# Turning expert 0's first rows earlier, casting two weights later, and filling both banks of a PSUM pair in an attention and mixture-of-experts kernel

## The chip, the core and the metric

The kernel runs on one core of a Trainium2 chip. The metric is device time in microseconds, the median of several runs. A core has five engines that each work through a queue of their own, strictly in order: TensorE (PE, matrix products; its weight loads are listed apart as PEld), VectorE (DVE), ScalarE (ACT), GpSimd (POOL) and SyncE (SP, which here only issues DMA transfers). They meet through counting semaphores: an instruction whose input is not ready holds up everything behind it on its own engine, and nothing on the others. Matrix products are summed in PSUM, which this kernel cuts into eight banks of 128 partitions x 512 float32 values.

## The reference

Three stages, each feeding the next, in float32 to the accuracy of float32:

```python
# 1 attention: batch 4, 8 heads, 576 tokens, head size 64
scores = (q @ k.T) / 8
keep   = scores >= scores.max(-1) - tau
attn   = softmax(where(keep, scores, -1e9));  x = attn @ v        # -> 2304 rows x 512
# 2 mixture of experts: 8 experts, two per row, hidden size 1024
noisy  = x @ w_gate + log1p(exp(x @ w_noise)) * noise
top2, top2_w = the two largest of noisy, softmax over the two
out[r] = sum over its two experts e of top2_w * (relu(x[r] @ w1[e]) @ w2[e])
# 3 a dense layer: hidden size 2048
h = out @ w_in;  y = (max(h, 0) + alpha * min(h, 0)) @ w_out
```

## The kernel before

Each operand of a product of the second and third stage, and of the scores, is held as two parts, a high one (a cast to fp32r) and a low one (the original minus the high part), and each product is summed from three: high x high, high x low, low x high. The high part is a cast on ScalarE, the low part a subtraction on VectorE or GpSimd.

**Attention.** The work is cut into 80 units (`units`): a batch, a chunk of 128 query rows, a pair of heads. A loop over iterations `i` overlaps four stages of different units, and what each engine does is emitted in exactly the order in which the loop is written (the schedule is manual). In iteration `i`:

- `t_mm(i-2, part)` transposes the masked exponentials of unit i-2 on TensorE in three parts (L418, L418, L420), and `a2` copies each part out of PSUM on ScalarE (L430, L430, L432);
- `d1(i, h)` on VectorE scales the scores of the two heads and takes their minimum (L377); `a1(i, h)` on ScalarE forms the two exponentials (L388);
- `d2(i-1, h)` on VectorE masks and sums the exponentials of the unit before (L401, two instructions); the transposes of the next iteration need them;
- `s_mm(i+1)` on TensorE computes the next unit's scores (L362) into two pairs of PSUM banks (`ps_s`); the pairs are freed by `d1(i)`;
- `pv(i-3)` multiplies with V (L454, L456).

After a chunk's last pair of heads a tile of 128 rows of attention output is complete: it is copied out of PSUM (`group_evac`, L479), turned (`turn_rows`, L497), divided by its sum (`scale_rows`, L505), and its gate logits are made (L522, L527, L531, L535, L538). Per group of one to three tiles the gate is then evaluated in a chain of small instructions (`gating`: L564 to L616) that ends in the rank of each row within its expert (L601 to L606 on TensorE, L612, L614 on VectorE) and in an indirect DMA that scatters the rows to their experts (L637).

**What is added to the loop by a table.** `put(i, f)` adds work `f` to iteration `i`; `put((i, p), f)` says where: p = -1 is ahead of `d2`, 0 ahead of `pv`, 1 at the end (the default). Two things are put there ahead of the next stage. The first eight weight blocks of expert 0 are loaded, cast (`w_hi`, L171 on ScalarE, 128 x 1024) and subtracted (`w_lo`, L177 on GpSimd, two instructions), one block in every second iteration from 66. And expert 0's first 256 rows, complete by then, are loaded in iteration 70 (`x_load`) and turned in iterations 78 and 79 (`x_split`: four transposes at L203 on TensorE, then the high half at L206 on ScalarE and the low half at L207 on VectorE).

**Fill.** From iteration 80 on there are no new scores to compute, and TensorE is given the first block of expert 0: eight sums of 12 matmuls over those 256 rows (`first_1`, L214, output 128 x 256), each followed by a cast with relu on ScalarE (`relu`, L224) and a subtraction on VectorE (L225), and then `first_2` (L232) for the second weight matrix. They run between and behind the last attention units, so that TensorE has work while the gate of the last tiles is evaluated and their rows are scattered and read back. The order is: sums 0 and 1 in iterations 80 and 81, sum 2, the last but one `pv`, sum 3 in iteration 82, and sums 4 to 7 among the last tile's logits and rank.

**PSUM.** `psum_s()` hands out a pair of banks as one tile, of which there are two; `psum_t()` one bank, of which there are three; `psum_v()` one. When a buffer comes round again, its first writer is made to wait for the last reader of what was there before. `first_1` takes a new pair for each sum and uses one bank of it, so the sums go round over two pairs, and sum f waits for the reads of sum f-2.

Of the kernel before, what the change touches and what calls it, by code (L numbers as in the profile page):

```python
# [14 lines left out]
HP = H // 2  # L15
# [4 lines left out]
NT = N // 128  # L20
# [5 lines left out]
DT = 2  # L26
# [7 lines left out]
def emit(tc, qt, kt, v, tau, wg, wn, noise, w1, w2, w_in, w_out, alpha, out):  # L34
# [8 lines left out]
    with (  # L43
# [59 lines left out]
        def psum_t(dt=FT):  # L103
            return pp.tile([128, 512], dt, name="ps_t", tag="t", bufs=3)
# [75 lines left out]
        xrows = {}  # L180
# [16 lines left out]
        def x_split(src, j, x, bank=None, is_blocked=True):  # L197
            ps = (bank or (psum_v, psum_t, psum_t, psum_t)[j])()
            if is_blocked:
                dve.transpose(ps, src)  # L200
            else:
                for c in range(HP):
                    pe.transpose(ps[:, c * 128:c * 128 + 128], src[:, c * 128:c * 128 + 128], ident)  # L203
            pv_ = ps.rearrange("p (c t) -> p c t", c=HP)
            xh = x[0][:, :, j * 128:j * 128 + 128]
            act.copy(xh, pv_)  # L206
            dve.tensor_tensor(x[1][:, :, j * 128:j * 128 + 128], pv_, f32(xh), op=OP.subtract)  # L207
# [139 lines left out]
        NU = len(units)  # L347
# [136 lines left out]
        def x_stages(T):  # L484
# [31 lines left out]

            def logits_mm():
                x = xts[T]
                ps = psum_t()
                g["lp"] = ps  # L520
                for c in range(HP):
                    pe.matmul(ps[c * 32:c * 32 + 32, :128], wcat[:, c], x[:, c], start=True, stop=True,  # L522
                              skip_group_check=True)
# [16 lines left out]
            if T < NT - 2:  # L540
                return [(0, 1, turn_rows), (1, -1, scale_rows), (1, 1, logits_mm), (2, -1, logits_copy),
                        (2, 1, flip), (3, -1, sum_)]
            return [(0, 1, rows), (1, 1, logits), (2, 1, flip), (3, 0, sum_), (0, 0, inverse)]

        def bc8(ap, n):
# [173 lines left out]
        put(64, w_load, 1)  # L719
        for n in range(W0):  # L720
            i = 66 + 2 * n
            put(i, w_hi, n)
            put(i + 1, w_lo, n, pool)
            put(i + 1, w_load, n + 2)
        for t in range(BLOCK0 // 128):
            put(70, x_load, 0, t)
            put(NU - 4 + DT + t, lambda t: x_split(xrows.pop((0, t)), t, X0, psum_t, False), t)

        fill = []

        def first_1(f):
            ps = psum_s()[:, f % 2]
            relu(f, BLOCK0, mm1(ps, BLOCK0, [0, 1, 2, 3], X0, f * 128), H0)

        g2 = {}
# [22 lines left out]
        for i in range(END):  # L758
# [32 lines left out]
            if outs:  # L791
                pv(iv)
                if units[iv][2] == HP - 1 or iv < SOLO:
                    T = group_evac(iv)
                    if T is not None:
                        todo = [(i + (1, 3, 5, 7, 2)[T] + d if T < 5 else i + 1 + d, p, f) for d, p, f in x_stages(T)]
                        if T == NT - 1:
                            last_rows.append(todo[0][2])
                            todo = [(i + 1, 0, todo[1][2]), (i + 1, 0, todo[4][2]), (i + 2, 0, todo[2][2]), (i + 2, 0, todo[3][2])]
                        if T == NT - 2:  # L800
                            todo = [(i + d, p, f[2]) for (d, p), f in zip(((1, 1), (1, 1), (2, 1), (2, 1)), todo)]
                        for t0, t1 in GROUPS:
                            if T == t1 - 1:
                                todo += [(i + {3: 8, NT - 1: 3, NT: 2}.get(t1, 4) + d, p, f) for d, p, f in gating(t0, t1)]
                        for j, p, f in todo:
                            put((j, p), f)
# [390 lines left out]
```

## Time and profile before

| | |
|---|---|
| median of 3 runs | 1158.6 us (1158.15 to 1158.63) |
| the profiled execution's own time | 1154.86 us |
| its span | 1153.1 us |
| TensorE busy | 1126.6 us, 98% |
| VectorE busy | 624.7 us, 54% |
| ScalarE busy | 529.1 us, 46% |
| GpSimd busy | 532.9 us, 46% |
| granted clock of TensorE | 0.9 or more in each of 40 slices |

Times in the profile run from the start of the span. The end of the span lies 1.8 us short of the execution's own time. Iteration 74 of the attention loop ends at about 270 us, iteration 78 at 287 us; the last attention product ends at 305 us, the gate of the last tile at 316 us, and the 1153 us end with the dense layer. A timeline row gives the start, the duration, the engine, the line and operation, the names and the shape, how many instructions of a kind were merged (x4), and in brackets the idle time of the engine just before the first of them with what ended it. Ends of matmuls are modelled and overlap the next start.

### The profile page before, as it was taken

The page shows a single profiled execution, that of the slowest core. Times are in us where ns is not written, and L with a number is a line of the kernel's source. Part 1 is how long each engine was busy: PE and PEld are TensorE (multiplying, and loading weights), DVE is VectorE, ACT ScalarE, POOL GpSimd, SP SyncE. Part 2 cuts the span into 40 slices and gives each one's busy share as a digit, 9 for nine tenths or more (in the row PEclk, how much of TensorE's full clock was granted, in tenths as well). Part 3 has the DMA queues.
Part 4 walks back from the last instruction along what each step waited for, and adds up shares of the span by engine and source line. Part 5 has one row for each costly group of instructions (what it writes and reads, how often), then busy time and mean ns, then how long its engine had stood idle before and what let it go on. Part 6 is the DMA issues. An engine that isn't in the chain of part 4 may idle for free. (4 is left out here: it accounts for less than half of the span.)

```text
span 1153.1 us, 20565 instructions
## 1 busy us (share of the span) xinstructions
PE 1126.6 (98%) x7754; PEld 973.3 (84%) x7754; DVE 624.7 (54%) x1332; ACT 529.1 (46%) x1039; POOL 532.9 (46%) x632
## 2 busy tenths in 40 slices
PE   7999999999899999999999999999999999999997
PEld 6887887877798989888989999898888888888886
DVE  6979999898534544454444444444443442442221
ACT  7978888788434444454444444433111121121111
POOL 7746545653525455545555455475332332332221
PEclk9999999999999999999999999999999999999999
DMA  6524222232356767677667675632321321320001
GB/s 211 150 87 126 92 96 84 93 120 93 147 157 190 201 193 197 191 186 196 192 187 200 195 202 168 188 120 69 77 53 50 75 57 45 80 57 20 24 1 39
DMA packets 156552, 141.50 MB, mean 123 GB/s; under 512 B 108576, under 2 KB 109216, under 8 KB 156448
## 3 DMA queue, kind: packets, MB, share of 16 engines
q1 hardware_dynamic: 150400, 120.91, 35.9%
q0 software_dynamic: 5760, 18.88, 4.9%
q8 instruction: 63, 1.03, 0.4%
q14 instruction: 41, 0.34, 0.1%
q10 hardware_dynamic: 288, 0.34, 0.1%
HBM read 97.11 MB, written 42.99 MB: 121 GB/s over the span
## 5 line engine op out<-in xcount | busy, mean ns | idle before, releaser
L214 PE MATMUL ps_t<-m_v,m_pair 128*128 128x384 f32 (+2 forms) x1216 | 220.1, 317 | 0.3 <-DVE m_v L207 0.3
L177 POOL TENSOR_TENSOR m_pair<-m_v,m_pair 128x512 fp32r<-128x512 f32 x114 | 151.7, 1352 | 129.5 <-ACT m_pair L171 107.5
L214 PEld LDWEIGHTS ps_t<-m_v,m_pair 128*128 128x128 f32 x1216 | 186.8, 190 | 8.4 <-DVE m_v L207 0.5
L1018 DVE TENSOR_SCALAR m_tmp<-ps_t,alpha_t 128x512 f32<-128x512 f32 (+1 forms) x80 | 55.7, 696 | 209.2 <-PE ps_t L214 207.3
L232 PE MATMUL ps_s<-m_pair,m_hh 128*128 128x512 f32 x528 | 167.4, 390 | 0.0
L225 DVE SCALAR_TENSOR_TENSOR m_gate<-ps_t,m_hh 128x384 fp32r<-128x384 f32 (+1 forms) x120 | 58.8, 492 | 169.4 <-ACT m_hh L224 169.3
L214 PE MATMUL ps_t<-m_v,m_early 128*128 128x256 f32 (+2 forms) x672 | 127.3, 320 | 0.0
L401 DVE SCALAR_TENSOR_TENSOR m_hh<-m_tmp,sm,m_hh 128x576 f32<-128x576 f32 x144 | 125.4, 903 | 0.0
L377 DVE TENSOR_SCALAR_CACHE_REDUCE m_tmp<-ps_s 128x576 f32<-128x576 f32 x144 | 105.2, 752 | 23.4 <-ACT m_last L432 9.0
L232 PEld LDWEIGHTS ps_s<-m_pair,m_hh 128*128 128x128 f32 x528 | 99.1, 188 | 20.3
L1023 POOL TENSOR_TENSOR m_v<-m_tmp,m_v 128x512 fp32r<-128x512 f32 x39 | 50.4, 1294 | 140.1 <-ACT m_v L1022 140.1
L214 PEld LDWEIGHTS ps_t<-m_v,m_early 128*128 128x128 f32 x672 | 105.9, 189 | 5.1 <-DVE m_v L207 0.4
L388 ACT ACTIVATE m_hh<-m_tmp,sm 128x576 f32<-128x576 f32 x144 | 105.6, 781 | 4.9 <-DVE m_tmp L377 4.8
L1022 ACT CAST m_v<-m_tmp 128x512 fp32r<-128x512 f32 x39 | 24.2, 621 | 173.7 <-DVE m_tmp L1019 173.7
L232 PE MATMUL ps_s<-m_pair,m_gate 128*128 128x512 f32 x264 | 102.9, 390 | 0.0
L362 PE MATMUL ps_s<-m_pair 64*128 64x288 f32 (+1 forms) x864 | 88.9, 318 | 12.2 <-DVE m_tmp L377 7.1
L224 ACT ACTIVATE m_hh<-ps_t 128x384 fp32r<-128x384 f32 (+1 forms) x120 | 52.7, 439 | 98.2 <-PE ps_t L214 96.8
L1023 POOL TENSOR_TENSOR m_gate<-m_tmp,m_gate 128x512 fp32r<-128x512 f32 (+1 forms) x41 | 44.1, 1076 | 115.8 <-ACT m_gate L1022 109.6
L1042 PE MATMUL ps_s<-m_pair,m_v 128*128 128x512 f32 x396 | 95.1, 389 | 0.0
L362 PEld LDWEIGHTS ps_s<-m_pair 64*128 64x128 f32 (+1 forms) x864 | 69.3, 192 | 26.0 <-DVE m_tmp L377 16.5
L1042 PE MATMUL ps_s<-m_pair,m_gate 128*128 128x512 f32 x360 | 88.3, 391 | 0.0
L1042 PEld LDWEIGHTS ps_s<-m_pair,m_v 128*128 128x128 f32 x396 | 74.3, 188 | 15.4
(233 smaller groups left out, 1981.3 us busy)
## 6 DMA issues: line engine op xcount, KB each, us to landing
m_v<-in_w_dram SPq DMA_DIRECT2D x64, 512.0 KB, 4.0
yg<-m_tmp SPq DMA_DIRECT2D x40, 256.0 KB, 3.3
m_tmp<-in_w_in_dram SPq DMA_DIRECT2D x16, 512.0 KB, 4.6
m_tmp<-in_w_out_dram SPq DMA_DIRECT2D x16, 512.0 KB, 5.2
m_early<-in_kt_dram SPq DMA_DIRECT2D x15, 320.0 KB, 3.4
yg<-m_gate SPq DMA_DIRECT2D x18, 256.0 KB, 2.1
m_rows<-xg SPq DMA_DIRECT2D x72, 64.0 KB, 2.8
out_dram<-m_tmp SPq DMA_DIRECT2D x18, 256.0 KB, 2.4
```

The source lines that it names most:

```text
L177: eng.tensor_tensor(WL[n][:, w], raw[:, w], f32(WH[n][:, w]), op=OP.subtract)
L214: pe.matmul(ps[:, :n], w[wc[d]][:, col:col + 128], x[xx][:, d, :n], start=(k == 0), stop=(k == 11))
L224: act.activation(h, ps, AF.Relu)
L225: dve.scalar_tensor_tensor(hs[1][:, f * n:f * n + n], ps, 0.0, f32(h), op0=OP.max, op1=OP.subtract)
L232: pe.matmul(ps, a[:, o:o + 128], ww[w][:, c:c + 512], start=(f == 0 and k == 0), stop=(f == nf - 1 and k == 2))
L362: pe.matmul(u["ps", h][:, x, :288], lhs, kk[r, o:o + 288], start=(k == 0), stop=(k == 2))
L377: dve.tensor_scalar(u["sp"][:, h].rearrange("p (a b) -> p a b", a=2), ps[:, :, :288], -0.125, None, op0=OP.mult, op1=OP.min, accum_out=u[" ...
L388: act.activation(u["em"][:, h], u["sp"][:, h], AF.Exp, bias=u["sm"][:, h:h + 1], scale=-1.0)
L401: dve.scalar_tensor_tensor(u["em"][:, h], u["sp"][:, h], sm[:, 2 + h:3 + h], u["em"][:, h], op0=OP.is_le, op1=OP.mult, accum_out=acc)
L1018: dve.tensor_scalar(g, ps, 0.0, alpha_t[:, f:f + 1], op0=OP.min, op1=OP.mult)
L1023: pool.tensor_tensor(h[:, n:2 * n], g, f32(h[:, :n]), op=OP.subtract)
L1042: pe.matmul(ps, h[x][:, t * 128:t * 128 + 128], ww[w][:, c:c + 512], start=(f == 0 and k == 0), stop=(f == 15 and k == 2))
```

## The change

Five edits to the table of work and to two helpers. Expert 0's two row tiles are turned at the end of iterations 74 and 78 instead of 78 and 79, and their halves are formed one iteration later at position -1, ahead of the masks `d2`. The casts, subtractions and following loads of weight blocks 6 and 7 move from iterations 78 to 81 to iterations 80 and 81. The logits of the last but one tile use a `ps_s` pair and have their stages listed one by one. `first_1` takes a new pair only for every second sum and puts two sums into its two banks.

```diff
@@ -201,6 +201,9 @@
             else:
                 for c in range(HP):
                     pe.transpose(ps[:, c * 128:c * 128 + 128], src[:, c * 128:c * 128 + 128], ident)
+            x_halves(ps, j, x)
+
+        def x_halves(ps, j, x):
             pv_ = ps.rearrange("p (c t) -> p c t", c=HP)
             xh = x[0][:, :, j * 128:j * 128 + 128]
             act.copy(xh, pv_)
@@ -516,7 +519,7 @@
 
             def logits_mm():
                 x = xts[T]
-                ps = psum_t()
+                ps = psum_s()[:, 0] if T == NT - 2 else psum_t()
                 g["lp"] = ps
@@ -540,6 +543,9 @@
             if T < NT - 2:
                 return [(0, 1, turn_rows), (1, -1, scale_rows), (1, 1, logits_mm), (2, -1, logits_copy),
                         (2, 1, flip), (3, -1, sum_)]
+            if T == NT - 2:
+                return [(0, 1, turn_rows), (0, 1, logits_mm), (1, -1, logits_copy), (1, 0, scale_rows),
+                        (1, 1, flip), (1, 1, sum_)]
             return [(0, 1, rows), (1, 1, logits), (2, 1, flip), (3, 0, sum_), (0, 0, inverse)]
@@ -719,17 +725,28 @@
         for n in range(W0):
             i = 66 + 2 * n
-            put(i, w_hi, n)
-            put(i + 1, w_lo, n, pool)
-            put(i + 1, w_load, n + 2)
+            put(i if n < 6 else (NU + n - 6, 0), w_hi, n)
+            put(i + 1 if n < 6 else NU + n - 6, w_lo, n, pool)
+            put(i + 1 if n < 6 else NU + n - 6, w_load, n + 2)
+        x0_bank = {}
+
+        def x0_turn(t):
+            x0_bank[t] = psum_t()
+            src = xrows.pop((0, t))
+            for c in range(HP):
+                pe.transpose(x0_bank[t][:, c * 128:c * 128 + 128], src[:, c * 128:c * 128 + 128], ident)
+
         for t in range(BLOCK0 // 128):
             put(70, x_load, 0, t)
-            put(NU - 4 + DT + t, lambda t: x_split(xrows.pop((0, t)), t, X0, psum_t, False), t)
+            put(74 + 4 * t, x0_turn, t)
+            put((75 + 4 * t, -1), lambda t: x_halves(x0_bank[t], t, X0), t)
 
         def first_1(f):
-            ps = psum_s()[:, f % 2]
+            if f % 2 == 0:
+                g2["up"] = psum_s()
+            ps = g2["up"][:, f % 2]
             relu(f, BLOCK0, mm1(ps, BLOCK0, [0, 1, 2, 3], X0, f * 128), H0)
@@ -797,8 +814,6 @@
-                        if T == NT - 2:
-                            todo = [(i + d, p, f[2]) for (d, p), f in zip(((1, 1), (1, 1), (2, 1), (2, 1)), todo)]
```

The new lines shift the numbers: what is L377 and L401 before is L380 and L404 after, L206 and L207 become L209 and L210, L214 and L225 become L217 and L228.

The first place is VectorE in iterations 74 to 76. `sm_149` to `sm_152` belong to units 73 to 76; the rows with `m_hh` are the masks, those with `ps_s` the scaled scores. Before:

```order
L535 TENSOR_TENSOR m_rows<-ps_t,es_144 128x128
L538 TENSOR_REDUCE m_rows<-m_rows 128x16
L401 SCALAR_TENSOR_TENSOR m_hh,es_146<-m_tmp,sm_149,m_hh 128x576 x2
L377 TENSOR_SCALAR m_tmp,sm_151<-ps_s 128x576 x2
L401 SCALAR_TENSOR_TENSOR m_hh,es_146<-m_tmp,sm_150,m_hh 128x576 x2
L377 TENSOR_SCALAR m_tmp,sm_152<-ps_s 128x576 x2
```

And now, at the same place on VectorE:

```order
L538 TENSOR_TENSOR m_rows<-ps_t,es_144 128x128
L541 TENSOR_REDUCE m_rows<-m_rows 128x16
L404 SCALAR_TENSOR_TENSOR m_hh,es_146<-m_tmp,sm_149,m_hh 128x576 x2
L380 TENSOR_SCALAR m_tmp,sm_151<-ps_s 128x576 x2
L210 TENSOR_TENSOR m_pair<-ps_t,m_pair 128x4x128
L404 SCALAR_TENSOR_TENSOR m_hh,es_146<-m_tmp,sm_150,m_hh 128x576 x2
L380 TENSOR_SCALAR m_tmp,sm_152<-ps_s 128x576 x2
```

The low half of the first row tile (L210) now stands between unit 75's scores and unit 74's masks; in iteration 79 the second one stands likewise between unit 79's scores and unit 78's masks.

The second place is ScalarE in iteration 75. L171 is weight block 4's cast, L564 belongs to a gate, L430 and L432 copy the transposes of unit 73, L388 is unit 75's two exponentials. Before:

```order
L171 CAST m_pair<-m_v_73 128x1024
L564 ACTIVATE m_gate<-m_rows 128x24
L430 COPY m_last<-ps_t 128x512
L388 ACTIVATE m_hh<-m_tmp,sm_151 128x576 x2
L430 COPY m_last<-ps_t 128x512
L382 ACTIVATE sm_151<-sm_151,taut 128x2
L432 COPY m_last<-ps_s 128x128
```

And now on ScalarE:

```order
L171 CAST m_pair<-m_v_73 128x1024
L570 ACTIVATE m_gate<-m_rows 128x24
L433 COPY m_last<-ps_t 128x512
L391 ACTIVATE m_hh<-m_tmp,sm_151 128x576 x2
L209 CAST m_pair<-ps_t 128x4x128
L433 COPY m_last<-ps_t 128x512
L385 ACTIVATE sm_151<-sm_151,taut 128x2
L435 COPY m_last<-ps_s 128x128
```

The high half of the row tile (L209), which L210 on VectorE reads, stands behind the two exponentials and ahead of the copy of unit 73's second part. In iteration 79 it is the same with `sm_155`, and the weight cast that stood in iteration 78 is gone from there.

The third place is TensorE in the fill, sums 5, 6 and 7, with the semaphore that a row waits for (`DVE_49` counts VectorE's instructions). The number behind `ps_s` names the PSUM tile. Before:

```order
L214 MATMUL ps_s_4554<-m_pair_72,m_early_3500 128x256 [waits DVE_49]
L214 MATMUL ps_s_4554<-m_pair_72,m_early_3500 128x256 x8
L214 MATMUL ps_s_4554<-m_pair_72 128x256 x3
L214 MATMUL ps_s_4569<-m_pair_72,m_early_3500 128x256 [waits DVE_49]
L214 MATMUL ps_s_4569<-m_pair_72,m_early_3500 128x256 x8
L214 MATMUL ps_s_4569<-m_pair_72 128x256 x3
L214 MATMUL ps_s_4584<-m_pair_72,m_early_3500 128x256 [waits DVE_49]
L214 MATMUL ps_s_4584<-m_pair_72,m_early_3500 128x256 x8
L214 MATMUL ps_s_4584<-m_pair_72 128x256 x3
```

And now on TensorE:

```order
L217 MATMUL ps_s_4512<-m_pair_72,m_early_3500 128x256 [waits DVE_49]
L217 MATMUL ps_s_4512<-m_pair_72,m_early_3500 128x256 x8
L217 MATMUL ps_s_4512<-m_pair_72 128x256 x3
L217 MATMUL ps_s_4566<-m_pair_72,m_early_3500 128x256 x9
L217 MATMUL ps_s_4566<-m_pair_72 128x256 x3
L217 MATMUL ps_s_4566<-m_pair_72,m_early_3500 128x256 [waits DVE_49]
L217 MATMUL ps_s_4566<-m_pair_72,m_early_3500 128x256 x8
L217 MATMUL ps_s_4566<-m_pair_72 128x256 x3
```

Before, each of the three sums has a tile of its own and waits for VectorE's read of the sum two places back (7 for the read of 5). Now the even sums wait for nothing, and an odd sum waits: the count it asks for is that of VectorE's read (L228) of the even sum just ahead of it, which lies in the other bank of the same tile (7 waits for the read of 6, 5 for that of 4, and 3, in tile `ps_s_4447`, for that of 2).

## Rows read from the trace of the kernel before

**Rows 1.** Busy us (x instructions) of PE, PEld, DVE, ACT, POOL in two stretches:

```profile
281.00:318.00 37.00, 32.32 (x324) 27.50 (x321) 22.76 (x88) 17.21 (x43) 17.98 (x31) 1.00 0.34 129
345.00:700.00 355.00, 354.70 (x1989) 322.82 (x1988) 168.93 (x277) 165.49 (x276) 184.13 (x140) 1.00 0.68 194
```

**Rows 2.** Waits of TensorE, 240 to 320 us: total, times, longest:

```profile
PE ps_s L362 <- DVE m_tmp L377: 2.0, 7, 0.3
```

**Rows 3.** Waits of TensorE, 318 us to the end, all there are:

```profile
PE ps_t L214 <- DVE m_v L207: 0.3, 1, 0.3
```

**Rows 4.** Timeline of TensorE, 275 to 296 us:

```profile
275.32 1.06 PE L362 MATMUL ps_s<-m_pair 64*128 64x288 f32 x12 [0.18 <-DVE m_tmp L377]
...
287.04 0.64 PE L418 MATMUL ps_t<-ident,m_hh 128*128 128x128 f32 x4
289.09 0.66 PE L418 MATMUL ps_t<-ident,m_hh 128*128 128x128 f32 x4 [1.42 <-ACT m_last L430]
289.59 0.27 PE L420 MATMUL ps_t<-ident,m_hh 128*128 128x128 f32 x1
...
291.03 0.66 PE L203 MATMUL ps_t<-ident,m_v 128*128 128x128 f32 x4
291.96 0.66 PE L497 MATMUL ps_t<-ident,m_last 128*128 128x128 f32 x4 [0.27 <-ACT m_last L430]
...
293.36 1.09 PE L418 MATMUL ps_t<-ident,m_hh 128*128 128x128 f32 x8 [0.39 <-ACT m_rows L527]
...
295.00 1.09 PE L454 MATMUL ps_v<-m_last,m_v 128*64 128x128 f32 x16
```

**Rows 5.** Timeline of TensorE, starts of sums 3 and 7:

```profile
304.89 1.34 PE L214 MATMUL ps_s<-m_pair,m_early 128*128 128x256 f32 x9
...
313.72 1.34 PE L214 MATMUL ps_s<-m_pair,m_early 128*128 128x256 f32 x9 [1.64 <-DVE m_pair L225]
```

**Rows 6.** Timeline of VectorE, 256 to 290 us:

```profile
256.15 1.83 DVE L401 SCALAR_TENSOR_TENSOR m_hh<-m_tmp,sm,m_hh 128x576 f32<-128x576 f32 x1
...
270.44 0.76 DVE L377 TENSOR_SCALAR_CACHE_REDUCE m_tmp<-ps_s 128x576 f32<-128x576 f32 x1
...
271.12 0.82 DVE L401 SCALAR_TENSOR_TENSOR m_hh<-m_tmp,sm,m_hh 128x576 f32<-128x576 f32 x1
...
271.86 0.82 DVE L401 SCALAR_TENSOR_TENSOR m_hh<-m_tmp,sm,m_hh 128x576 f32<-128x576 f32 x1
...
274.50 0.76 DVE L377 TENSOR_SCALAR_CACHE_REDUCE m_tmp<-ps_s 128x576 f32<-128x576 f32 x1 [1.13 <-ACT m_last L432]
...
275.18 0.67 DVE L490 TENSOR_SCALAR es<-es 128x8 f32<-128x8 f32 x1
...
288.58 0.69 DVE L207 TENSOR_TENSOR m_pair<-ps_t,m_pair 128x512 fp32r<-128x512 f32 x1 [2.35 <-ACT m_pair L206]
289.19 0.75 DVE L377 TENSOR_SCALAR_CACHE_REDUCE m_tmp<-ps_s 128x576 f32<-128x576 f32 x1
```

**Rows 7.** Timeline of ScalarE, iterations 75 and 79:

```profile
272.19 1.45 ACT L388 ACTIVATE m_hh<-m_tmp,sm 128x576 f32<-128x576 f32 x2
273.53 0.58 ACT L430 COPY m_last<-ps_t 128x512 f32<-128x512 f32 x1
...
287.96 0.59 ACT L206 CAST m_pair<-ps_t 128x512 fp32r<-128x512 f32 x1
288.44 0.60 ACT L430 COPY m_last<-ps_t 128x512 f32<-128x512 f32 x1
```

**Rows 8.** Timeline of GpSimd, subtractions of weight blocks 2 and 4:

```profile
256.07 3.04 POOL L177 TENSOR_TENSOR m_early<-m_v,m_early 128x512 fp32r<-128x512 f32 x2 [5.27 <-ACT m_early L171]
...
273.32 2.50 POOL L177 TENSOR_TENSOR m_pair<-m_v,m_pair 128x512 fp32r<-128x512 f32 x2
```

**Rows 9.** Timeline of VectorE, reads of sum 2, and of 5 with 6:

```profile
305.54 0.42 DVE L225 SCALAR_TENSOR_TENSOR m_pair<-ps_s,m_pair 128x256 fp32r<-128x256 f32 x1
...
313.24 0.75 DVE L225 SCALAR_TENSOR_TENSOR m_pair<-ps_s,m_pair 128x256 fp32r<-128x256 f32 x2
```

## The prediction

> **What bounds the kernel now.** I read the page's busy times first (TensorE 98%), then the busy times by stretch, to see where the missing 2% lies. From 345 to 700 us TensorE has no gap worth naming; from 281 to 318 us it is busy for 32.32 of 37.00 us [rows 1]. The change touches 270 to 318 us only, so at most some 5 us are to be won, and what is lost there stays lost: the list of waits from 318 us to the end has one entry for TensorE's products, 0.3 us [rows 3], so nothing later can take up a delay.
>
> Next the list of waits of TensorE for 240 to 320 us, then its timeline, to see which waits end last. Three kinds matter. While the attention loop is full, TensorE's scores wait for VectorE seven times, 0.3 us at the longest, 2.0 us together [rows 2]: the two engines run level, and a delay of VectorE there is one of TensorE. In iterations 79 and 80 there are waits of 1.42, 0.27 and 0.39 us [rows 4]; in the first of them ScalarE is working off a weight cast and a row tile's half ahead of the copy that TensorE needs. In the fill, sum 7 waits 1.64 us for VectorE's read of sum 5 [rows 5], which stands behind the last gate's small instructions and starts at 313.24 [rows 9].
>
> **Term A, the first row tile's halves in iteration 75: +2.4 us, and +0.5 for a collision.** Before, VectorE goes from unit 75's scores straight to unit 74's masks, at 271.12 [rows 6]. Now the subtraction of the low half comes first, and it needs ScalarE's cast. ScalarE comes to that cast only behind unit 75's exponentials: it takes the place that the copy has now, at 273.53 [rows 7]. It lasts 0.59 us, like the cast at 287.96 [rows 7], until 274.12; VectorE's subtraction followed 0.03 us behind such a cast (287.96 + 0.59 to 288.58), and the next instruction 0.61 us behind its start [rows 6, 7]. So the masks start at 274.15 + 0.61 = 274.76 instead of 271.12. Two masks at a spacing of 0.74 (271.12 to 271.86) lead to 276.24; two scores at 0.68 (270.44 to 271.12), the second lasting 0.76, end at 276.92 + 0.76 = 277.68. Before, the same second score began at 274.50, behind an idle 1.13 us that swallows part of the delay, and ended at 275.26. The lag is 2.4 us, and TensorE's next scores, which started 0.06 us behind it at 275.32 [rows 4], move by as much. The four transposes themselves, some 0.5 us at the end of iteration 74, vanish in this wait.
>
> The collision: unit 74's first mask would now start at 274.76, within GpSimd's subtraction of weight block 4, 273.32 to 275.82 [rows 8]. A mask that started at 256.15, within the one at 256.07, took 1.83 us instead of 0.82 [rows 6, 8]: +1.0. Against that, the small instruction at 275.18, 0.67 us long and ending as GpSimd does, falls behind it and may lose up to 0.5. I take +0.5 and keep -0.5 to +1.0 for the range.
>
> **Term B, iterations 78 to 80: -0.2 us.** Two things leave ScalarE's queue, a weight cast in iteration 78 and one row half; two things come back. The second tile's half again stands behind two exponentials, and the copy of unit 77's second part behind that half, and the third part's transposes wait for a bank that this copy frees (of the three single banks the row tile and the last rank hold one each meanwhile). From the start of the first transposes at 287.04 to the product at 295.00 it is 7.96 us now [rows 4]. Then: 0.64 for the transposes [rows 4] and 0.05 to the copy; 0.48 (287.96 to 288.44) for a copy in the queue; 1.34 for the exponentials (272.19 to 273.53); 0.48 for the half; 0.60 for the second copy [rows 7] and 0.05 to the third transposes: 3.64 us until these start. From their start, 289.59, to 295.00 it was 5.41 us, of which the turn at 291.03 to 291.69, the 0.27 behind it and the 0.39 go [rows 4]: 4.09. Together 7.73, a gain of 0.2 us. VectorE idles there as before (2.35 us, [rows 6]), now for the second tile. If no copy were late, all three waits, 2.1 us, would go; if the wait behind the turn stays, +0.1. The other edits here cost nothing on the path: weight casts 6 and 7 now run while ScalarE waits for the fill's sums, and block 6's products come after 316 us; GpSimd's first two scatters go ahead and the next two wait for block 6, but rows are read back only after the last scatter, which waits for the last rank. The last but one tile's logits use a pair that is free from iteration 80 on; its division by the sums is put behind unit 79's masks, where VectorE has room. If weight block 7's subtraction slides into the next gate on VectorE, up to 0.8 us of that gate's small instructions could wait (the spread of the 0.67 above); I leave it to the range.
>
> **Term C, the paired sums: +1.4 us.** A pair is meant to keep sum 7 from waiting for the read of 5. The order shows what it waits for now: the read of 6, which stands one place further back in the same queue. Likewise sum 3 waits for the read of 2, and 5 for that of 4. Sum 3 started at 304.89 [rows 5]; the read of sum 2 stands behind a gate on VectorE and ran from 305.54 to 305.96 [rows 9]. With 0.06 us for the semaphore, sum 3 starts 1.1 us later, and with it everything that follows: the logits of the last tile, its gate, its scatter. Sum 5 loses some more, but sum 7 is held by the last gate anyway. The reads of 5 and 6 ran from 313.24 to 313.99 [rows 9] and sum 7 started at 313.72 [rows 5]; now it starts 0.06 behind the second, +0.3 on top of the 1.1. So the wait of 1.64 us is not removed. The bounds: 1.1 if sum 6's read is early, 2.2 with the gate delayed by block 7.
>
> The sum against the profiled execution: 2.4 + 0.5 - 0.2 + 1.4 = +4.1 us, its 1154.86 becoming 1159.0 and its span of 1153.1 becoming 1157.2. The runs' median is 1158.6, 3.7 us above that execution; the same shift gives 1162.7. With the outer terms, 1.9 to 3.4 for A, -1.0 (half of the three waits) to +0.1 for B, 1.1 to 2.2 for C, it is +2.0 to +5.7.
>
> **Rivals.** First: the two banks are independent, and the third edit does what its name says. The wait of 1.64 us goes, sum 3 is not delayed: A + B - 1.6 = +1.1, 1159.7 us. For it speaks that the reads and the next sum touch different banks; against it the wait that the built program carries on every odd sum. The Trainium skill takes its side: in "PSUM — Partial Sum Buffer", section "Summary: rules for kernel authors", whoever reads PSUM while a product runs is to have the product go to a different bank, with the guard set by bank. By that rule alone sum 3 could start with the read of 2 still out, and the time would be this rival's; no run here shows it, as the guard in this program is set by tile.
>
> Second, on the other side: TensorE has work in hand in iterations 75 to 77, so that VectorE's late masks are covered. It decides from the point where TensorE is more than 2.4 us ahead of VectorE. Then A is 0, B is the whole 2.1 us of waits, and C stays: -2.1 + 1.4 = -0.7, 1157.9 us, not slower. For it speaks VectorE's idle 1.13 us and its 2.35 us; against it the seven waits for scores, which show no lead at all.
>
> Third: VectorE and GpSimd collide at every chance, in iteration 75 and again in the gate at 303 us: the upper bounds, +5.7, 1164.3 us.
>
> **Chances.** The forecast 74%, the first rival 8%, the second 7%, the third 8%; 3% for a gain that I see no way to. A measurement of this kernel can tell about 0.2%, 2.3 us, from no change. The forecast's own lower end, +2.0, is just inside that, so a few hundredths of its chance fall there: slower 0.80, same 0.17, faster 0.03. The range for 8 in 10 goes from 1159.7, which takes in the first rival, to 1164.6, just beyond the third.
>
> **What would show it.** VectorE's row half in iteration 75 with an idle of about 3.0 us ahead of it, waiting for ScalarE's cast (271.15 to 274.15), and TensorE waiting some 2.4 us more in iteration 76 than now. In iteration 79 TensorE waiting twice, for the second and the third transposes, and no longer at the division's transposes. Sums 3, 5 and 7 each waiting for VectorE's read of their neighbour, sum 7 for about as long as now. Wrong would be: no idle of VectorE ahead of that half (term A falls), odd sums without a wait (term C falls), or a gap of TensorE behind 318 us that takes the delay up.

## The result and the profile after

The changed kernel takes 1164.86 us (1163.71 to 1166.36, 6 runs) against 1158.46 us (1157.93 to 1159.28, 6 runs) of the kernel before on the same chip: +6.4 us, ratio 1.0056, 95% interval 1.0043 to 1.0069. It is slower, as forecast, by more than the +4.1 us forecast; 1164.86 lies 0.26 us above the range.

The profiled execution takes 1163.71 us, span 1162.0, which is 8.9 us more than the span of before. 2.75 us of that lie ahead of everything that was changed. The list of TensorE's waits of the kernel after, 100 to 262 us, shows a wait of more than 1 us on each of two lines:

```profile
PE ps_s L365 <- DVE m_tmp L380: 4.6, 12, 1.1
...
PE ps_t L534 <- ACT m_rows L530: 1.2, 1, 1.2
```

They belong to the chip, not to the change. The profiled execution of the kernel before lacks them, and so do those of the eight runs below on two chips where the kernel before takes 1154.6 us; all eight on two chips where it takes 1159 us have both, whichever edits they carry. So from here on spans are not compared. I measure five stages of TensorE's timeline from a common mark, the turn of logits that ends iteration 73 (L531 before, L534 after): to the scores of unit 79, to the first sum, to sum 3, to the second weight matrix, to block 1's first sum. Before they take 18.53, 12.06, 8.64, 10.46 and 12.50 us; after 20.62, 13.21, 10.65, 11.37 and 12.64. The sum is +6.30, near the +6.4 of the medians.

**Iterations 74 to 79: +2.1 us.** ScalarE's timeline, then VectorE's, then TensorE's, answering to [rows 4, 6, 7]:

```profile
274.95 1.45 ACT L391 ACTIVATE m_hh<-m_tmp,sm 128x576 f32<-128x576 f32 x2
276.29 0.58 ACT L209 CAST m_pair<-ps_t 128x512 fp32r<-128x512 f32 x1
```

```profile
276.90 0.69 DVE L210 TENSOR_TENSOR m_pair<-ps_t,m_pair 128x512 fp32r<-128x512 f32 x1 [2.93 <-ACT m_pair L209]
277.51 1.06 DVE L404 SCALAR_TENSOR_TENSOR m_hh<-m_tmp,sm,m_hh 128x576 f32<-128x576 f32 x1
...
280.60 0.16 DVE L493 TENSOR_SCALAR es<-es 128x8 f32<-128x8 f32 x1
```

```profile
278.72 1.31 PE L421 MATMUL ps_t<-ident,m_hh 128*128 128x128 f32 x8 [1.46 <-DVE m_hh L404]
280.05 0.33 PE L423 MATMUL ps_s<-ident,m_hh 128*128 128x128 f32 x1
280.73 1.06 PE L365 MATMUL ps_s<-m_pair 64*128 64x288 f32 x12 [0.35 <-DVE m_tmp L380]
```

VectorE stands idle for 2.93 us until the cast behind two exponentials is done, and TensorE waits 1.46 us for the masks behind it. From the mark the scores of unit 77 start 12.32 us on, against 9.66. Of these 2.66 us the next scores get 0.5 back: the small instruction that took 0.67 beside GpSimd takes 0.16 now.

**Iteration 79 to the first sum: +1.15 us.** TensorE's timeline, and its busy time and granted clock (the third number) in three stretches:

```profile
293.25 0.65 PE L421 MATMUL ps_t<-ident,m_hh 128*128 128x128 f32 x4 [0.73 <-ACT m_last L433]
295.55 0.47 PE L423 MATMUL ps_t<-ident,m_hh 128*128 128x128 f32 x1 [1.64 <-ACT m_last L433]
295.95 1.98 PE L457 MATMUL ps_v<-m_tmp,m_v 128*64 128x128 f32 x16
```

```profile
286.00:295.00 9.00, 6.72 (x77) 1.00 0.17 60
295.00:299.00 4.00, 3.45 (x26) 0.57 0.16 66
299.00:305.00 6.00, 5.63 (x59) 1.00 0.22 87
```

The two waits are the forecast ones. Behind the second the granted clock is halved (1.2 instead of 2.4 GHz) for some 3 us: 16 products take 1.98 us instead of 1.09 [rows 4]. No step of the prediction had this.

**The sums: +2.0 us to sum 3, +0.9 behind it.** VectorE's timeline before (one line) and after, then GpSimd's, the odd sums of TensorE's, and ScalarE's cast of sum 6, answering to [rows 5, 8, 9]:

```profile
303.07 0.17 DVE L569 TENSOR_SCALAR m_gate<-m_gate 128x16 f32<-128x16 f32 x1
```

```profile
309.07 1.05 DVE L575 TENSOR_SCALAR m_gate<-m_gate 128x16 f32<-128x16 f32 x1
...
312.42 0.42 DVE L228 SCALAR_TENSOR_TENSOR m_pair<-ps_s,m_pair 128x256 fp32r<-128x256 f32 x1
```

```profile
307.52 2.55 POOL L177 TENSOR_TENSOR m_pair<-m_v,m_pair 128x512 fp32r<-128x512 f32 x2
```

```profile
312.89 1.33 PE L217 MATMUL ps_s<-m_pair,m_early 128*128 128x256 f32 x9 [1.94 <-DVE m_pair L228]
...
317.59 1.33 PE L217 MATMUL ps_s<-m_pair,m_early 128*128 128x256 f32 x9 [0.39 <-DVE m_pair L228]
...
320.19 0.52 PE L217 MATMUL ps_s<-m_pair 128*128 128x256 f32 x3
322.63 1.34 PE L217 MATMUL ps_s<-m_pair,m_early 128*128 128x256 f32 x9 [1.92 <-DVE m_pair L228]
```

```profile
321.74 0.38 ACT L227 ACTIVATE m_pair<-ps_s 128x256 fp32r<-128x256 f32 x1 [2.04 <-PE ps_s L217]
```

All three odd sums wait for the read of their neighbour, sum 7 longer than before (1.64, [rows 5]). The gate's first small instruction takes 1.05 us, not 0.17; it ends at 310.12, as GpSimd's subtraction of weight block 7 does (310.07). Ahead of sum 7 something else is late: the last matmul of sum 6 ends at 320.71 (320.19 + 0.52), but ScalarE's cast of that sum, which VectorE's read follows, starts only at 321.74, 1.03 us behind this modelled end. Behind 318 us TensorE waits twice, for the 1.9 us of sum 7 and the 0.3 us of [rows 3]: nothing takes the delay up.

### The profile page after: what moved, and what is told of

Same layout as the page of the kernel before. It is cut to its first block, busy times and chain, and to the rows that moved or that the text cites. A ratio compares the mean times of both kernels' runs of the same rounds, so it can differ in the third digit from the quotient of the medians.

```text
span 1162.0 us, 20569 instructions
## 1 busy us (share of the span) xinstructions
PE 1128.7 (97%) x7754; PEld 974.2 (84%) x7754; DVE 624.6 (54%) x1332; ACT 529.6 (46%) x1039; POOL 531.5 (46%) x632
## 3 DMA queue, kind: packets, MB, share of 16 engines
q8 instruction: 63, 1.03, 0.4%
## 5 line engine op out<-in xcount | busy, mean ns | idle before, releaser
L217 PE MATMUL ps_t<-m_v,m_pair 128*128 128x384 f32 (+2 forms) x1216 | 220.1, 317 | 0.3 <-DVE m_v L210 0.3
L217 PEld LDWEIGHTS ps_t<-m_v,m_pair 128*128 128x128 f32 x1216 | 186.9, 190 | 8.4 <-DVE m_v L210 0.5
L228 DVE SCALAR_TENSOR_TENSOR m_gate<-ps_t,m_hh 128x384 fp32r<-128x384 f32 (+1 forms) x120 | 58.9, 493 | 169.0 <-ACT m_hh L227 168.9
L217 PE MATMUL ps_t<-m_v,m_early 128*128 128x256 f32 (+2 forms) x672 | 127.2, 320 | 0.0
L404 DVE SCALAR_TENSOR_TENSOR m_hh<-m_tmp,sm,m_hh 128x576 f32<-128x576 f32 x144 | 125.8, 906 | 0.0
L380 DVE TENSOR_SCALAR_CACHE_REDUCE m_tmp<-ps_s 128x576 f32<-128x576 f32 x144 | 105.2, 753 | 25.1 <-ACT m_last L435 8.5
L217 PEld LDWEIGHTS ps_t<-m_v,m_early 128*128 128x128 f32 x672 | 105.9, 189 | 5.0 <-DVE m_v L210 0.2
```

What stands on the lines that cost most here:

```text
L217: pe.matmul(ps[:, :n], w[wc[d]][:, col:col + 128], x[xx][:, d, :n], start=(k == 0), stop=(k == 11))
L228: dve.scalar_tensor_tensor(hs[1][:, f * n:f * n + n], ps, 0.0, f32(h), op0=OP.max, op1=OP.subtract)
L380: dve.tensor_scalar(u["sp"][:, h].rearrange("p (a b) -> p a b", a=2), ps[:, :, :288], -0.125, None, op0=OP.mult, op1=OP.min, accum_out=u[" ...
L404: dve.scalar_tensor_tensor(u["em"][:, h], u["sp"][:, h], sm[:, 2 + h:3 + h], u["em"][:, h], op0=OP.is_le, op1=OP.mult, accum_out=acc)
```

## The experiments

Each compares with the kernel before on its own chip, medians of up to 31 runs. The stages are the five above, in us over before, from one profiled execution each; a run's median can differ from its sum of stages by 1 us or more. The column "us" is not comparable from row to row, since the kernel before takes 1154.6 us on the chips of the first four and the last four runs and 1159 us on those of the eight between.

| run | us | over before | ratio, 95% interval | stages |
|---|---|---|---|---|
| paired sums alone | 1156.23 | +1.6 | 1.0004 to 1.0022 | 0, 0, +1.1, +0.3, 0 |
| early turns alone | 1157.86 | +3.2 | 1.0015 to 1.0035 | +2.1, +1.05, 0, 0, +0.1 |
| casts alone | 1153.66 | -1.0 | 0.9983 to 1.0002 | 0, -0.9, 0, 0, 0 |
| logits alone | 1153.76 | -0.9 | 0.9986 to 1.0004 | 0, -0.45, 0, 0, 0 |
| pairs and casts | 1161.38 | +2.3 | 1.0014 to 1.0033 | 0, -0.9, +1.9, +1.7, +1.0 |
| split halves | 1161.33 | +2.3 | 1.0012 to 1.0030 | +0.5, -2.2, +2.0, +1.1, 0 |
| casts and logits | 1158.11 | -0.9 | 0.9983 to 1.0001 | 0, -1.3, 0, +0.4, 0 |
| all but pairs | 1162.88 | +3.8 | 1.0022 to 1.0049 | +2.5, -0.2, 0, +0.4, +0.3 |
| free pairs | 1158.28 | -0.6 | 0.9986 to 1.0004 | 0, 0, 0, -1.6, +1.2 |
| split halves, free pairs | 1156.84 | -2.1 | 0.9974 to 0.9992 | +0.5, -2.2, 0, -1.2, +1.5 |
| one filler | 1164.28 | +5.4 | 1.0032 to 1.0060 | +2.6, -0.2, +2.0, +1.1, 0 |
| changed kernel again | 1165.71 | +6.8 | 1.0042 to 1.0070 | +2.1, +1.4, +2.0, +2.3, 0 |
| split turns alone | 1153.62 | -1.0 | 0.9984 to 1.0002 | +0.5, -1.5, 0, 0, 0 |
| block 7 on VectorE | 1159.54 | +5.0 | 1.0026 to 1.0054 | +2.1, +1.35, +1.1, +0.3, 0 |
| two fillers | 1160.22 | +5.6 | 1.0033 to 1.0060 | +2.1, -0.2, +2.0, +1.75, +0.2 |
| all cures | 1151.43 | -3.2 | 0.9962 to 0.9983 | +0.5, -2.2, 0, -1.6, +0.2 |

### One edit at a time

The runs carry the hunks of the change singly: the pairing of `first_1`; `x0_turn` and `x_halves`; the three `put` lines of blocks 6 and 7; the two hunks on the logits.

> The kernel before with the third edit alone: block 0's sums in pairs in one PSUM tile. Theory (an odd sum waits for VectorE's read of the even one, because the two lie in one tile): TensorE waits ahead of sums 3 and 7, +1.1 to +1.7 in the gate and +0.3 to +0.9 behind it, together +1.4 to +2.3 us; the subtraction of weight block 7 is in its old place here, so the gate's first small operation stays at 0.17 us. Rival (the waits come only from what the casts do to the gate): within 0.3 us of before, and no wait ahead of sum 3.

> The kernel before with the early turns alone (transposes of expert 0's first two row tiles in iterations 74 and 78, their halves ahead of the masks of iterations 75 and 79); casts, last logits and sums as before. Theory (VectorE's half stands ahead of the masks and waits for ScalarE's cast behind two exponentials): VectorE stands idle 2 to 3 us ahead of the first half, TensorE is 2.1 to 2.9 us later at iteration 77's scores, and the total is +1.5 to +3.0 us, since the turns come out of the tail. Rival (the lag is made by the moved casts): within 0.5 us of before or faster.

> The kernel before with weight blocks 6 and 7 cast behind the last exponentials alone. Theory (VectorE's first small operation of the gate meets GpSimd's subtraction of block 7, and in the kernel after this makes an odd sum wait): the gate's first operation takes about 1 us instead of 0.17, but with the sums in tiles of their own nothing on TensorE waits for it at once: 0 to +0.8 us. Rival (the casts leave ScalarE and GpSimd free for iterations 74 to 80): -0.5 to -1.0 us.

> The kernel before with the edit of the last but one token tile's logits alone (another PSUM tile and other places in iterations 78 to 80). Theory (it only moves four small matmuls): -0.3 to +0.3 us. Rival (it holds a tile of two banks that the scores of iteration 79 or 80 need): +0.5 to +1.2 us, as the 1.2 us that the changed kernel lost between iterations 78 and 80.

The first theory holds with its numbers; TensorE's timeline of the paired sums alone, sums 3 and 7:

```profile
305.76 1.34 PE L214 MATMUL ps_s<-m_pair,m_early 128*128 128x256 f32 x9 [1.05 <-DVE m_pair L225]
...
314.93 1.33 PE L214 MATMUL ps_s<-m_pair,m_early 128*128 128x256 f32 x9 [1.33 <-DVE m_pair L225]
```

The early turns alone bring the lag and, in this execution too, the halved clock (0.66 from 292 to 297 us); they cost slightly more than expected. The casts alone shorten the wait of [rows 4] from 1.42 to 0.73 us. The gate's first instruction takes 0.91 us there too, and no sum waits for it: both halves of that theory hold, but the time leans to the rival's gain. The logits alone take the 0.39 us wait away. For these two -0.9 us is within the uncertainty; for the logits neither expectation has it. The four add up to +2.9, not +6.4: the edits act on each other.

### Two and three edits together

> The kernel before with the moved weight casts and the paired sums, without the early turns and the logits edit. Theory (the two edits make each other dearer: with block 7's subtraction beside the gate, VectorE reads the even sum later, and the odd sum in the same tile waits for that): the wait ahead of sum 3 grows from the 1.27 us of the paired sums alone to 1.9 to 2.2 us, and the total is +1.7 to +2.2 us. Rival (the edits add up, +1.6 and -1.0): +0.4 to +0.8 us, sum 3 waiting 1.3 us.

> The kernel before with the moved weight casts and the logits edit, without the early turns and the pairing. Theory (they shorten two different waits between iterations 79 and the first sum, the copy behind the weight cast and the transposes behind the logits): -1.3 to -1.9 us. Rival (both shorten one wait): -0.8 to -1.0 us.

> The whole changed kernel with block 0's sums in tiles of their own, as before. Theory (what the early turns cost hides all that the casts and the logits edit give, since TensorE then waits for something else): +3.0 to +3.6 us, no wait ahead of sum 3 though the gate's first operation still takes about 1 us. Rival (the single edits add up: +3.2, -1.0, -0.9): +1.0 to +1.6 us.

The pairs with the casts cost +2.3 us where the single runs add up to +0.6; sum 3 waits 1.80 us and starts 1.9 us later than before, against 1.05 and 1.1 with the pairs alone. Sum 7 waits 2.09 us for a late cast of sum 6 (1.19 us behind the sum), after which TensorE's clock is halved there (0.66 from 320 to 325 us). Casts and logits together give -0.9, within the uncertainty and at the rival's end. The stage to the first sum has the theory's -1.3; 0.4 us is lost again behind sum 3, where ScalarE's copy of the attention output starts 1.42 us behind its last product (0.04 in the casts alone, on another chip, which lose nothing there). All but the pairs costs +3.8, a little over the range: with the early turns in place, the gain of the other two edits is gone, as the second and third transposes of iteration 79 now wait for ScalarE's queue instead. This execution has its halved clock in iteration 76 (0.68 from 281 to 286 us) and not in 79, and its stage to the first sum is -0.2.

### The halves at another place

```diff
-            put((75 + 4 * t, -1), lambda t: x_halves(x0_bank[t], t, X0), t)
+            put((75 + 4 * t, 1), lambda t: x_halves(x0_bank[t], t, X0, (0,)), t)   # the cast
+            put((76 + 4 * t, -1), lambda t: x_halves(x0_bank[t], t, X0, (1,)), t)  # the subtraction
```

> The whole changed kernel, but ScalarE's cast of a turned row tile stands at the end of iterations 75 and 79 and VectorE's subtraction ahead of the masks of iterations 76 and 80, when the cast is long done. Theory (the cost is VectorE idling for a cast behind two exponentials): VectorE's idle time ahead of both subtractions is gone, iteration 77's scores are 0.5 to 1.2 us late instead of 2.65, TensorE's clock stays at 1.00 before the first sum, and the total is +3.0 to +4.5 us over before instead of +6.4. Rival (the cost is the turned rows' hold on one of three PSUM banks of tag t, which now lasts longer): transposes of iterations 75, 76 and 79 wait more, and the total stays at +5.5 us or more.

> The kernel before with the early turns alone, their halves split as in the run of split halves (cast at the end of iterations 75 and 79, subtraction ahead of the masks of 76 and 80). Theory (turning early takes the turns and a bank's wait out of the tail, once nothing stalls on the halves): +0.5 us at iteration 79's scores and -1.0 to -2.2 us from there to the first sum, total -0.5 to -1.7 us. Rival (the gain needs the logits edit or the moved casts as well): 0 to +0.6 us.

VectorE's timeline of the whole changed kernel with split halves: the subtraction has no idle time of its own, and the 1.02 us ahead of it is the wait that the kernel before has at this place (1.13, [rows 6]).

```profile
278.78 0.76 DVE L382 TENSOR_SCALAR_CACHE_REDUCE m_tmp<-ps_s 128x576 f32<-128x576 f32 x1 [1.02 <-ACT m_last L437]
...
279.46 0.69 DVE L212 TENSOR_TENSOR m_pair<-ps_t,m_pair 128x512 fp32r<-128x512 f32 x1
```

The second subtraction still waits, 1.62 us, but behind the last scores. The lag is 0.5 us, and the stage to the first sum 2.2 us under before: turning early does gain. The total, +2.3, is under the range expected. The rival is there in a small way, one wait of 0.98 us in iteration 76 for the bank. Turned alone, two instructions at another place are worth 4.2 us: +3.2 with the halves ahead of the masks, -1.0 split (this last by itself within the uncertainty, and the first with a halved clock in it).

### The pairs without the wait

```diff
+            if f % 2:
+                for m in last_mm:                 # the odd sum's 12 matmuls
+                    for r in last_read:           # the cast and the subtraction of the even one
+                        tc.declare_no_dep(m.ins, r.ins, reason="the other bank of the pair")
```

> The kernel before with the paired sums alone, and with the dependency between an odd sum's matmuls and the reads of the even sum in the other bank of its tile declared absent. Theory (the wait is the program's bookkeeping by tiles, not the chip's banks): no wait ahead of sums 3, 5 and 7, the 1.64 us that sum 7 waits in the kernel before is gone too, total -1.3 to -1.7 us, against the +1.6 us of the paired sums with the dependency. Rival (writing one bank while its neighbour is read slows either): odd sums or VectorE's reads take longer, total 0 to +1.6 us.

> The whole changed kernel with both cures: halves split over two iterations, and odd sums that do not wait for the even one's reads. Theory: the 2.2 us that the split halves gained before the first sum, less 0.5 us of lag, plus 1.6 us at the sums, less about 0.4 us for the gate's meeting with block 7's subtraction: -2.5 to -3.5 us against before. Rival (the sums then wait for weights or for VectorE elsewhere): -1.0 to -1.8 us.

TensorE's timeline of the free pairs alone, sums 3 and 7 and the first of the two matmuls of the gate's last check:

```profile
309.77 1.34 PE L216 MATMUL ps_s<-m_pair,m_early 128*128 128x256 f32 x9
...
316.80 1.24 PE L216 MATMUL ps_s<-m_pair,m_early 128*128 128x256 f32 x9
...
320.98 0.18 PE L625 MATMUL ps_t<-m_gate 128*128 128x8 bf16 x1 [0.70 <-DVE m_gate L618]
```

No sum waits, and VectorE's read of sum 2, from 310.42 us on, falls within sum 3, whose first nine matmuls take 1.34 us, as they do before [rows 5]: the two banks are independent on the chip, and the wait was the program's bookkeeping by tile. "PSUM — Partial Sum Buffer" of the Trainium skill, section "Summary: rules for kernel authors", tells whoever reads PSUM while a matmul runs to target a different bank and to guard by bank; this run agrees. But of the 1.6 us won at the sums 1.2 are given back: the second weight matrix takes 13.7 us instead of 12.5. Of these, 0.9 are at the gate's last check, which TensorE now reaches before VectorE does; here too VectorE is later by a cast of sum 6 that starts 1.83 us behind its sum. So -0.6, within the uncertainty, where -1.3 to -1.7 was expected. With the split halves it is -2.1, short of the theory's -2.5: 1.5 us are given back in the second weight matrix, and 0.4 are lost behind sum 3, as with casts and logits.

### Weight block 7 beside the gate

In the whole changed kernel:

```diff
-            put(i + 1 if n < 6 else NU + n - 6, w_lo, n, pool)
+            if n == 7:
+                put((NU + 1, 0), w_lo, n, dve)
+            else:
+                put(i + 1 if n < 6 else NU, w_lo, n, pool)
```

> The whole changed kernel with weight block 7's subtraction on VectorE, in the 3.3 us that it stands idle ahead of the gate, instead of on GpSimd beside the gate. Theory (GpSimd's subtraction holds up the gate's first operation): that operation takes 0.17 us again, sum 3 waits 1.2 to 1.4 us instead of 2.15, and the total is 0.9 to 1.5 us under the changed kernel, +4.9 to +5.5 us over before. Rival (the gate is late for another reason): sum 3 still waits 1.9 us or more, total +6 us or more.

VectorE's timeline, then TensorE's sums 3 and 7:

```profile
304.42 1.23 DVE L177 TENSOR_TENSOR m_pair<-m_v,m_pair 128x1024 fp32r<-128x1024 f32 x1 [1.38 <-ACT m_pair L171]
...
306.69 0.17 DVE L575 TENSOR_SCALAR m_gate<-m_gate 128x16 f32<-128x16 f32 x1
```

```profile
309.62 1.34 PE L217 MATMUL ps_s<-m_pair,m_early 128*128 128x256 f32 x9 [1.05 <-DVE m_pair L228]
...
318.79 1.34 PE L217 MATMUL ps_s<-m_pair,m_early 128*128 128x256 f32 x9 [1.32 <-DVE m_pair L228]
```

The gate's first instruction is at 0.17 us again, and sums 3 and 7 wait as long as in the paired sums alone. But this run and the changed kernel's were on different chips. The two fillers, described next, ran on this chip with the subtraction beside the gate; TensorE's sums 3 and 7 and the cast of sum 6 there:

```profile
308.66 1.48 PE L217 MATMUL ps_s<-m_pair,m_early 128*128 128x256 f32 x9 [1.93 <-DVE m_pair L228]
...
317.41 0.52 PE L217 MATMUL ps_s<-m_pair 128*128 128x256 f32 x3
319.24 1.34 PE L217 MATMUL ps_s<-m_pair,m_early 128*128 128x256 f32 x9 [1.31 <-DVE m_pair L228]
```

```profile
317.96 0.38 ACT L227 ACTIVATE m_pair<-ps_s 128x256 fp32r<-128x256 f32 x1 [1.05 <-PE ps_s L217]
```

So the subtraction beside the gate costs 0.9 us at sum 3, and no cost of it shows at sum 7. The other 0.6 us at sum 7 come with the late cast of sum 6.

This cast starts 0.03 or 0.04 us behind its sum in the kernel before and in all eight runs on the chips of 1154.6 us. It starts 1.0 to 2.1 us behind it in the changed kernel and in all eight on the chips of 1159 us, the free pairs among them, which leave the weight casts in their old place. Where each sum has a tile of its own nothing is lost by it: in casts and logits and in all but the pairs the cast is 2.0 and 2.1 us late, and sum 7 starts 3.27 and 3.24 us behind sum 6, against 3.25 in the kernel before. With the pairs, sum 7 waits for the read behind it. Why the cast is late is open: the profile shows no work of ScalarE ahead of it, and since ends of matmuls are modelled, the sum itself may end later than its row says.

"SBUF — State Buffer" of the Trainium skill, section "SBUF: two separate sides", describes an exclusive lock on a pair of ports that VectorE and GpSimd share, held for a whole instruction; the gate's instruction of 1.05 us in the changed kernel, which ended 0.05 us behind GpSimd's, agrees.

### The halved clock

```diff
+            if i == NU - 4:                     # second run only, ahead of t_mm(it, 0)
+                for c in range(9):
+                    pe.transpose(st[i]["ps", 0][:, 0, 384:], ident, ident)
+            if i == NU - 1:                     # both runs, ahead of t_mm(it, 2)
+                spare = psum_s()
+                for c in range(10):
+                    pe.transpose(spare[:, 0, :128], ident, ident)
```

> The whole changed kernel with ten transposes of the identity into an unused bank, put ahead of the third transposes of iteration 79, where TensorE waits 1.64 us; their output is not read. Theory (TensorE's clock is halved because the engine stood idle there): the granted clock stays at 1.00 between 290 and 300 us, the 20 attention-value matmuls behind the wait take 1.24 us instead of 2.33, and the total is 0.8 to 1.3 us under the changed kernel, so about +5 to +5.5 us over before. Rival (the clock falls for another reason, or the time is given back at the next wait): total as the changed kernel, +6 us or more.

> The whole changed kernel with work that nobody reads in both waits ahead of the sums: ten transposes of the identity in iteration 79 as in the first filler run, and nine ahead of the first transposes of iteration 76, where TensorE waits 1.46 us. Theory (the clock falls because the engine stands idle at one or the other of the two waits): the granted clock stays at 1.00 from 270 to 305 us, and the total is 0.9 to 1.5 us under the changed kernel, +4.9 to +5.5 us over before. Rival (the clock falls for a reason that filling does not touch): it is still halved for some 3 us between iterations 76 and 80, total +5.8 us or more.

> The changed kernel unaltered, on the same chip as the three others. Theory: +5.5 to +7.0 us over before, with TensorE's clock halved once or twice behind a wait between iterations 76 and the sums, not always at the same wait. Rival (the +6.4 us were those of one chip): under +4.5 us here.

TensorE's busy time and granted clock, first of one filler, then of two, then of the changed kernel again:

```profile
281.00:286.00 5.00, 4.63 (x45) 0.66 0.38 145
286.00:295.00 9.00, 8.31 (x104) 1.00 0.20 60
295.00:299.00 4.00, 3.20 (x35) 1.00 0.00 0
```

```profile
295.00:299.00 4.00, 3.71 (x45) 1.00 0.49 197
299.00:305.00 6.00, 5.85 (x58) 1.00 0.51 175
305.00:313.00 8.00, 6.07 (x56) 0.79 0.40 133
```

```profile
295.00:299.00 4.00, 2.36 (x23) 0.78 0.00 0
299.00:305.00 6.00, 5.71 (x56) 0.86 0.33 131
305.00:313.00 8.00, 7.26 (x78) 1.00 0.45 141
313.00:321.00 8.00, 6.26 (x45) 0.79 0.42 156
```

The fillers leave 0.55 us of the 1.64. With the one wait filled, the clock stayed up there but had already halved behind the wait of iteration 76; with both filled, it stayed at 1.00 to the end of the first sums and halved behind the wait of sum 3; unaltered, it halved at iteration 79 and at sum 3.

Six executions have, fillers aside, the same edits ahead of the first sum. Their stage to it is 11.85 or 11.86 us in the three without halving in it (one filler, two fillers, all but pairs) and 13.21, 13.42 and 13.41 in the three with it (the changed kernel twice, block 7 on VectorE): a halving costs 1.35 to 1.55 us there. In iteration 76 it costs less: the first stage is 0.4 to 0.6 us longer with it (all but pairs, one filler). The totals, +5.4 and +5.6, are 1.4 and 1.2 us under that of the unfilled kernel (the last on another chip), but inside its interval, and neither reaches its rival's time. The runs do not show that filling moves the halving, or that idle time alone causes it: all but the pairs, with neither wait filled, is also halved at iteration 76 and not at 79, and split halves has waits of 2 us at the sums and no halving at all. The changed kernel again is within its theory, with two halvings.

### All cures

Split halves, free pairs and block 7 on VectorE, and the gate's last check later:

```diff
-                    do_fill()
+                    for _ in range(3):
+                        do_fill()
                     close()
```

> Split halves and unhindered odd sums, with weight block 7's subtraction on VectorE ahead of the gate, and the gate's last check (two matmuls that wait 0.9 us for VectorE) behind two more steps of fill work. Theory (both remaining losses of the run with the two cures go): -2.8 to -3.6 us against before. Rival (the two losses are covered, or VectorE is now late for a sum): -1.6 to -2.3 us, as without them.

All of TensorE's waits from 262 to 345 us:

```profile
PE ps_t L425 <- DVE m_pair L212: 1.0, 1, 1.0
PE ps_s L369 <- DVE m_tmp L384: 0.7, 2, 0.3
PE ps_t L504 <- ACT m_last L437: 0.2, 1, 0.2
```

1151.43 us against 1154.59: -3.2 us, the ratio's interval wholly under 1. No sum waits, the clock is at 1.00 throughout, and the end of the second weight matrix has given back only 0.2. The cast of sum 6 is on time on this chip (0.04 us), which helps VectorE at the last check; how much of the gain over the free pairs is the later check and how much the chip is not shown. It beats both kernels.

## Why the prediction was right in kind and short in size

- **What bounds it** held: nothing after 318 us took up any of the delay.
- **Term A** (+2.9) held in mechanism: idle of VectorE 2.93 us for a forecast 3.0, scores of unit 77 +2.66. TensorE's waits in iteration 76 grew by 1.6 us (0.18 to 1.46 and 0.35), not 2.4, as the four transposes of the turn took 0.5 of it. By unit 79 only +2.1 are left; by luck the 0.8 us forecast too many made up for part of what was missing elsewhere. Its collision, taken as +0.5, was -0.3 (first mask 0.24 longer, the small instruction 0.5 shorter), inside its bounds.
- **Term B** (-0.2) was right as a sum of waits: -0.2 in each of the three executions without a halved clock in that stage. What it left out is the clock. The prediction put the two waits of iteration 79 in the sum at their length alone; here the products behind them then ran at half clock, another +1.35: this step failed, its -0.2 measured +1.15.
- **Term C** (+1.4) held for the paired sums by themselves, +1.1 and +0.3 to the tenth, +1.6 measured; in the changed kernel it measured +2.9. The other step that failed is the one that the prediction took out of the sum: "If weight block 7's subtraction slides into the next gate on VectorE, up to 0.8 us of that gate's small instructions could wait [...]; I leave it to the range." It does slide in, in all ten executions that have it moved and on GpSimd (0.91 to 1.06 us instead of 0.17), and costs 0.9 at sum 3. The last 0.6 are the late cast of sum 6, which no step of the prediction had. Both mattered only because the pairing had put a wait behind them.
- Together 2.1 - 0.2 + 1.35 + 1.5 + 0.9 + 0.6 = 6.25, against +6.30 in the stages and +6.4 measured. The range ended at the sum of the collisions, without a halved clock or a late cast, and so 0.26 us too low.
- **The first rival** (independent banks) was right about the chip and wrong about this program; once the program was told, the wait went. **The second** (TensorE in hand) fell with the wait of 1.46 us. **The third** (collisions everywhere) came closest by its time, 0.6 us under, but only the gate's collision was there.

What stays open is when the clock is halved, since the same wait at the same length had it behind it in one execution and not in another, and why the cast of sum 6 is late on some chips.

## What to carry to other kernels

An instruction put ahead of others in an in-order queue costs what its input is late, not what it takes: look up where that input stands in the other engine's queue, and move the consumer behind the moment it is ready (here 4.2 us for two subtractions and two casts, a halved clock included). Two edits that each cost or gain 1 us can make 0.9 us more together when one adds a wait and the other delays what is waited for; a collision next to a new wait belongs in the sum. And when a wait is taken away, look for the next instruction in the same queue that is early for the same engine: here the gate's last check took back more than half of the gain.

## What the runs showed of the hardware that was not expected

Behind waits of TensorE of 1.5 to 2.1 us in a stretch that was otherwise busy, the granted clock fell to half for about 3 us in eight of the profiled executions, at iteration 76, iteration 79, sum 3 or sum 7, and not at the same place each time for the same program; in the stage to the first sum that cost 1.35 to 1.55 us. Writing one bank of a PSUM pair while VectorE reads the other cost nothing: the first nine matmuls of sum 3 take 1.34 us with and without the read beside them. On two chips of four, and in the changed kernel's own execution, ScalarE's cast of sum 6 starts 1.0 to 2.1 us behind the modelled end of its sum, against 0.04 on the others, whichever edits the kernel carries.
